# Gated linear recurrence with a squared-ReLU feed-forward: longer units, Q~ and K~ transposed on VectorE, static buffers and a planned order

## Chip, cores and metric

The kernel runs on one core of one Trainium2 chip. The metric is device time in microseconds (us) of that core, the median of several runs. A profile is one further execution of the same program, recorded by the hardware profiler.

## The reference, cut to what matters

```python
# q, k, v, a_re, a_im: (B=4, H=8, S=768, D=48), float32
mag   = np.sqrt(a_re * a_re + a_im * a_im)
scale = np.minimum(mag, 0.999) / (mag + 1e-06)
a_re_n, a_im_n = a_re * scale, a_im * scale
for t in range(S):                       # S_re, S_im: (B, H, D, D), start at 0
    ar, ai = a_re_n[:, :, t, :, None], a_im_n[:, :, t, :, None]
    new_re = ar * S_re - ai * S_im
    new_im = ar * S_im + ai * S_re
    S_re, S_im = new_re + einsum('bhd,bhe->bhde', k[:, :, t], v[:, :, t]), new_im
    y[:, :, t] = einsum('bhd,bhde->bhe', q[:, :, t], S_re)
x = y.transpose(0, 2, 1, 3).reshape(3072, 384)
h = x @ w_in                             # w_in: (384, 2048), float64
return (relu(h) ** 2 @ w_out)            # w_out: (2048, 384), float64
```

The decay of a step is a complex number for each batch, head and feature. With its running product P_t, the step-by-step sum becomes a masked product of matrices: y_t is the sum over s up to t of (q_t P_t) against (k_s / P_s), times v_s. The kernel calls the two scaled operands Q~ and K~; each has a real and an imaginary part, so 96 rows for a head.

## The kernel before

**Tiling.** A unit is half a batch: L = 384 steps of all 8 heads, `W` = 3 blocks of 128 steps. There are 8 units. A unit goes through three stages.

**Chain** (`chain_work`, mostly VectorE and ScalarE). Partition p holds the steps 3p, 3p+1, 3p+2. `load` brings a_re, a_im, q, k (L643) and v (L654), on SP's queue for the first two units and POOL's afterwards. `roots` and `normalise` scale the decays (L668 to L696), `inner` multiplies the three steps of a partition together (L706 to L711), `inverse` forms 1/P within a partition (L717 to L731), `totals` transposes the partition totals on TensorE (L770) so that `scan` can run over the 128 partitions, which then lie along the free dimension; it does so by 16 calls of `product`, each one complex product in 4 VectorE operations (L799 to L803). `back` transposes the result back (L835, copied by ScalarE at L836), and `apply` multiplies everything out: 10 operations for each half of the heads (L847 to L862), which leave Q~ and K~ in the tile QK with steps on partitions.

**Pairs** (`pair_work`), for each of 4 pairs of heads. `turn` transposes Q~ and K~ on TensorE (L890, 12 for a pair) and ScalarE copies them to SBUF (L891) as QKT, features on partitions. `score` multiplies K~ by Q~ (L900) and VectorE masks the result (L902). `keep` forms each block's contribution to the state, K~ by v (L917), and VectorE adds them up (L925, L927). For that product K~ must lie with consecutive steps on partitions; `apply` gets it there over DRAM (rows<-QK at L869, KC<-rows at L871, both on POOL's queue). `mix` (L936, L941) adds masked scores by v and Q~ by state in `ypair`, ScalarE copies that out (L944), and SP moves the rows into `xT` (L952), where features are on partitions and steps along the row.

**Dense.** `hidden` computes one tile of 128 hidden features for 384 steps in three passes (L971), ScalarE applies ReLU and squares (L976, L977). `project` accumulates 16 tiles for 128 steps (L985), ScalarE copies out (L989), SP stores (L991). The weights arrive as float64. `fetch` (L581) loads raw pieces, 16 for each matrix, `lower` (L589, ScalarE) and `convert` (L602 to L609, VectorE) turn them into float32. `inspect` reads the weights once more late in the kernel (L624 to L629) and looks for exponents out of range; `verdict` (L1013 to L1032) puts all guard values into one flag. If the flag is set, `general_path` computes everything again by another method.

**Order.** Buffers come from rotating pools, and a framework inserts the waits. The order within an engine is that in which the Python code emits the work. `merge` (L1035) interleaves lists in proportion to their lengths: after a start by hand (chain 0, pairs 0 with the w_in conversion, chain 1 followed by the hidden tiles of unit 0, pairs 1 with the w_out conversion, chain 2), turn n merges the dense work of unit n with the pairs of unit n+1 and the chain of unit n+2.

Of the kernel before, what the change touches and what calls it, by code (L numbers as in the profile page):

```python
# [9 lines left out]
F32 = mybir.dt.float32  # L10
# [469 lines left out]

@with_exitstack
def fast_path(ctx, tc, q, k, v, a_re, a_im, moe_w_in, moe_w_out, out, flag):

# [7 lines left out]
    W = 3  # L496
    L = W * C
    NHALF = S // L
# [5 lines left out]
    NF = FF // C  # L504
    SCALE = 2.0 ** 59
    HH = H // 2
    NU = B * NHALF

    dve, pool, act = nc.vector, nc.gpsimd, nc.scalar

    const = ctx.enter_context(tc.tile_pool(name="const", bufs=1))
    nat = ctx.enter_context(tc.tile_pool(name="nat", bufs=1))
    wk = ctx.enter_context(tc.tile_pool(name="wk", bufs=1))
    pr = ctx.enter_context(tc.tile_pool(name="pr", bufs=2))
    gp = ctx.enter_context(tc.tile_pool(name="gp", bufs=NF // 2))
    xp = ctx.enter_context(tc.tile_pool(name="xp", bufs=2))
    NRAW = 5
    wst = ctx.enter_context(tc.tile_pool(name="wst", bufs=NRAW))
    trp = ctx.enter_context(tc.tile_pool(name="trp", bufs=2, space=PSUM))
    scp = ctx.enter_context(tc.tile_pool(name="scp", bufs=2, space=PSUM))  # L520
    dram = ctx.enter_context(tc.tile_pool(name="dram", bufs=1, space=bass.MemoryType.DRAM))
    yp = ctx.enter_context(tc.tile_pool(name="yp", bufs=1, space=PSUM))
    dp = ctx.enter_context(tc.tile_pool(name="dp", bufs=3, space=PSUM))

    act.preload_act_table_set("natural_log_exp_and_others")

    def after(x, y):

        tc.add_manual_dep(x.ins, y.ins.name, NOSYNC, reason="order")


    ident = const.tile([C, C], F32, name="ident")
    make_identity(nc, ident)

    mask = const.tile([C, C], F32, name="mask")
    pool.memset(mask, 1.0)
    pool.affine_select(out=mask, in_=mask, pattern=[[1, C]], compare_op=ALU.is_ge,
                       fill=0.0, base=0, channel_multiplier=-1)
    mask3 = mask.unsqueeze(1).to_broadcast([C, NM, C])

    sums = const.tile([C, NU, 7], F32, name="sums")
    mark = {}
    grow = const.tile([C, NU, NM], F32, name="grow")
    total = const.tile([C, B, NM], F32, name="total")

    ypair = yp.tile([C, L], F32, name="ypair")
    dve.memset(ypair, 0.0)


    w1 = const.tile([C, NF, NM, C], F32, name="w1")
    w2 = const.tile([C, NF, DM], F32, name="w2")

    wide = moe_w_in.dtype != F32
    odd = const.tile([C, 2 * NF], F32, name="odd")

    def piece(i):
        words = 2 if wide else 1
        if i < NF:  # L560
            w_in = moe_w_in.bitcast(U32) if wide else moe_w_in
            return (w1[:, i].rearrange("p m f -> p (m f)"),
                    w_in[:, ts(i, words * C)].rearrange("(m p) f -> p m f", p=C))
        i -= NF
        w_out = moe_w_out.bitcast(U32) if wide else moe_w_out
        return w2[:, i], w_out[ts(i, C), :].unsqueeze(1)

    raws = {}
    AHEAD = 3

    def fetch(i):

        dst, src = piece(i)
        if not wide:
            nc.gpsimd.dma_start(
                out=dst.rearrange("p (m f) -> p m f", m=src.shape[1]), in_=src)
            return

        raw = raws[i] = (gp.tile([C, DM, 2], U32, name="raw", tag="g") if i < NF else
                         wst.tile([C, DM, 2], U32, name="raw", tag="raw"))  # L580
        get = (nc.sync if i >= NF + NRAW else nc.gpsimd).dma_start(  # L581
            out=raw.rearrange("p (m f) two -> p m (f two)", m=src.shape[1]), in_=src)
        after(get, mark["landed"])

    def lower(i):

        if wide:
            lo = raws[i][:, :, 0]
            op = act.activation(out=lo, in_=lo, func=AF.Copy, scale=2.0 ** -29)  # L589
            after(op, mark["last"])  # L590

    def convert(i):

        for j in range(i, i + AHEAD) if i % NF == 0 else [i + AHEAD - 1]:
            if j // NF == i // NF:
                lower(j)
        if wide:
            dst, _ = piece(i)
            more, hi = raws[i][:, :, 0], raws[i][:, :, 1]
            bits = dst.bitcast(U32)  # L600

            first = dve.tensor_scalar(out=bits, in0=hi, scalar1=0x07FFFFFF, scalar2=3,  # L602
                                      op0=ALU.bitwise_and, op1=ALU.logical_shift_left)

            after(first, mark["QK", int(i >= NF + NRAW)])
            dve.scalar_tensor_tensor(out=bits, in0=hi, scalar=0xC0000000, in1=bits,
                                     op0=ALU.bitwise_and, op1=ALU.bitwise_or)

            dve.tensor_tensor(out=bits, in0=bits, in1=more, op=ALU.add)  # L609
        n = i + (NF // 2 if i < NF else NRAW)  # L610
        if n < (NF if i < NF else 2 * NF):
            fetch(n)

    SPARE = ("fa0", "fa1", "fb0", "fb1")

    def inspect(i):


        if not wide:
            return  # L620
        _, src = piece(i)
        t = wk.tile([C, 2, HH, W, D], F32, name="look", tag=SPARE[i % 4])
        flat_t = t.rearrange("p r h c d -> p (r h c d)").bitcast(U32)[:, 0:2 * DM]
        nc.gpsimd.dma_start(  # L624
            out=flat_t.rearrange("p (m f) -> p m f", m=src.shape[1]), in_=src)
        hi = flat_t.rearrange("p (n two) -> p n two", two=2)[:, :, 1]
        dve.tensor_scalar(out=hi, in0=hi, scalar1=0x38000000, scalar2=0x78000000,
                          op0=ALU.bitwise_xor, op1=ALU.bitwise_and)
        dve.tensor_reduce(out=odd[:, i:i + 1], in_=hi, axis=AX, op=ALU.max)  # L629


    def load(u):
        def src(ap):
            return ap[u["b"], :, ts(u["half"], L), :]


        get = nc.sync if u["n"] < 2 else nc.gpsimd
        for name, pair in (("a", (a_re, a_im)), ("qk", (q, k))):
            for z in range(2):
                t = u[name, z] = nat.tile([C, 2, HH, W, D], F32, name=f"{name}{z}",  # L640
                                          tag=f"{name}{z}")
                for j, ap in enumerate(pair):
                    get.dma_start(  # L643
                        out=t[:, j].rearrange("p h c d -> p h (c d)"),
                        in_=src(ap)[ts(z, HH)].rearrange(LOADS, c=W))
        if u["n"] == 0:

            gate = const.tile([C, 2], F32, name="gate")
            pool.tensor_copy(out=gate[:, 0:1], in_=u["a", 0][:, 1, HH - 1, W - 1, D - 1:D])
            mark["landed"] = pool.tensor_copy(out=gate[:, 1:2],  # L650
                                              in_=u["a", 1][:, 1, HH - 1, W - 1, D - 1:D])
        u["v"] = pr.tile([C, NM, H, D], F32, name="v", tag="v")
        for j in range(W):
            get.dma_start(out=u["v"][:, j],  # L654
                          in_=src(v).rearrange("h (j s) d -> s j h d", s=C)[:, j])

    def flat(t):
        return t.rearrange("p h c d -> p (h c d)")

    def whole(t):  # L660
        return t.rearrange("p r h c d -> p (r h c d)")

    def roots(u, z):

        a, n = u["a", z], u["n"]
        fa = u["fa", z] = wk.tile([C, 2, HH, W, D], F32, name=f"fa{z}", tag=f"fa{z}")
        fb = u["fb", z] = wk.tile([C, 2, HH, W, D], F32, name=f"fb{z}", tag=f"fb{z}")
        square = act.activation(out=whole(fa), in_=whole(a), func=AF.Square,  # L668
                                accum_out=sums[:, n, z:z + 1])
        m2 = flat(fb[:, 0])  # L670
        dve.tensor_tensor(out=m2, in0=flat(fa[:, 0]), in1=flat(fa[:, 1]), op=ALU.add)
        f0, f1, t = flat(fa[:, 0]), flat(fa[:, 1]), flat(fb[:, 1])
        act.activation(out=f0, in_=m2, func=AF.Ln)
        act.activation(out=f1, in_=f0, func=AF.Exp, scale=-0.5)
        last = act.activation(out=t, in_=f1, func=AF.Square)
        dve.scalar_tensor_tensor(out=t, in0=m2, scalar=-0.5, in1=t,
                                 op0=ALU.mult, op1=ALU.mult)
        dve.scalar_tensor_tensor(out=t, in0=t, scalar=1.5, in1=f1,
                                 op0=ALU.add, op1=ALU.mult)
        if n == 0 and z == 0:  # L680
            mark["roots"] = last
        elif n == 0:
            after(square, mark["roots"])
# [438 lines left out]
```

## Time and profile before

| What | Value |
|---|---|
| Runs | 807.89, 809.83, 813.04 us; median 809.83 |
| Span of the profiled execution | 808.9 us |
| Instructions in it | 9895 |
| DMA traffic | 76.24 MB, of which HBM read 56.62 and written 14.16 |
| POOL's DMA queues | 55.85 MB, 21.3% of 16 engines' span |
| SP's DMA queues | 19.67 MB, 8.2% |
| Chain that ended last, shares | PE 38%, issue 20%, VectorE 11%, DMA 10%, ScalarE 8% |

The costliest groups of instructions follow, from the page's fifth part: line, engine, operation, result and operands, shape and count, then busy us, mean ns of one, and the engine's idle time just before them with what ended it. A matmul row has a duration of its own, but matmuls overlap one another in the array, so a row's mean is longer than the distance from one to the next.

```profile
L971 PE MATMUL h<-xT,w 128*128 128x384 f32 x768 | 271.7, 496 | 4.7 <-DMA xT<-yt 3.2
L985 PE MATMUL o<-w,g 128*128 128x384 f32 x768 | 265.2, 493 | 0.0
...
L891 ACT COPY QKT<-tq 96x512 f32<-96x512 f32 x96 | 79.3, 851 | 34.6 <-PE tq L890 34.6
...
L890 PE MATMUL tq<-ident,QK 128*96 128x128 f32 x384 | 59.8, 289 | 21.5 <-DVE QK L862 14.9
```

### The profile page before, as it was taken

The numbers are of one execution on the slowest core, as the hardware profiler recorded it, in microseconds if no ns is written. First come the engines' busy times: TensorE is split into PE (matmuls) and PEld (weight loads), VectorE is DVE, ScalarE is ACT, GpSimd is POOL, SyncE is SP. The second block draws the span as 40 slices with busy tenths as digits, with TensorE's granted clock in tenths as the row PEclk, the third lists the DMA queues.
The fourth block names the chain that finished last, engine by engine and source line by source line (L and its number), as shares of the span: only waits on it lengthen the run. The fifth ranks groups of instructions, "written<-read, shape, count | busy, mean of one in ns | idle before, by whom it ended". The sixth has DMA issues, their size and how long they took to land.

```text
span 808.9 us, 9895 instructions
## 1 busy us (share of the span) xinstructions
PE 708.7 (88%) x3474; PEld 461.0 (57%) x3474; DVE 519.0 (64%) x1332; ACT 398.4 (49%) x753; POOL 110.2 (14%) x162
## 2 busy tenths in 40 slices
PE   0138794689899999999999998999999999899997
PEld 0027452665466666666666665666566666566554
DVE  5898899966987994639582866469464866600000
ACT  5814594435568618931586138811893145212510
POOL 5003100401030013000500031002300044200000
PEclk9998997789999999999999999999999999999999
DMA  9429310642043026000800053002600188500000
GB/s 278 151 69 327 92 59 1 223 132 57 11 142 107 18 68 203 9 8 28 266 22 7 18 172 100 8 17 80 219 9 16 28 280 270 196 17 28 1 12 23
DMA packets 38747, 76.24 MB, mean 94 GB/s; under 512 B 10752, under 2 KB 25216, under 8 KB 38688
## 3 DMA queue, kind: packets, MB, share of 16 engines
q0 software_dynamic: 14608, 55.85, 21.3%
q1 hardware_dynamic: 24080, 19.67, 8.2%
q8 instruction: 29, 0.48, 0.2%
q14 instruction: 30, 0.25, 0.1%
HBM read 56.62 MB, written 14.16 MB: 88 GB/s over the span
## 4 chain that ended last, share of the span: by engine, by line
PE 38%; issue 20%; DVE 11%; DMA 10%; ACT 8%; POOL 1%; SPq 0%; POOLq 0%; ACTq 0%
PE o L985 18%; PE h L971 11%; DVE fa L799 3%; DMA a<-in_a_im_dram 2%; PE sa L900 2%; DMA look<-in_moe_w_out_dram 2%; DMA look<-in_moe_w_in_dram 2%; PE ypair L936 1%; ACT QKT L891 1%; PE ypair L941 1%; PE kv L917 1%; DMA rows<-QK 1%; DMA KC<-rows 1%; PE tq L890 1%; ACT g L976 1%
## 5 line engine op out<-in xcount | busy, mean ns | idle before, releaser
L971 PE MATMUL h<-xT,w 128*128 128x384 f32 x768 | 271.7, 496 | 4.7 <-DMA xT<-yt 3.2
L985 PE MATMUL o<-w,g 128*128 128x384 f32 x768 | 265.2, 493 | 0.0
L985 PEld LDWEIGHTS o<-w,g 128*128 128x128 f32 x768 | 141.1, 192 | 85.8 <-issue 4.7
L971 PEld LDWEIGHTS h<-xT,w 128*128 128x128 f32 x768 | 140.2, 193 | 84.9 <-issue 8.6
L891 ACT COPY QKT<-tq 96x512 f32<-96x512 f32 x96 | 79.3, 851 | 34.6 <-PE tq L890 34.6
L976 ACT ACTIVATE g<-h 128x384 f32<-128x384 f32 x128 | 61.6, 484 | 55.8 <-PE h L971 55.5
L890 PE MATMUL tq<-ident,QK 128*96 128x128 f32 x384 | 59.8, 289 | 21.5 <-DVE QK L862 14.9
L890 PEld LDWEIGHTS tq<-ident,QK 128*96 128x96 f32 x384 | 46.6, 134 | 43.9 <-issue 26.7
L902 DVE TENSOR_TENSOR A<-sa,mask 128x384 f32<-128x384 f32 x64 | 35.2, 552 | 52.1 <-PE sa L900 52.0
L977 ACT ACTIVATE g<-g 128x384 f32<-128x384 f32 x128 | 66.4, 522 | 2.1
L900 PEld LDWEIGHTS sa<-QKT 96*128 96x128 f32 x384 | 52.5, 199 | 15.6 <-ACT QKT L891 5.6
L900 PE MATMUL sa<-QKT 96*128 96x128 f32 x384 | 57.2, 288 | 3.0 <-ACT QKT L891 3.0
L944 ACT COPY yt<-ypair 112x384 f32<-112x384 f32 x32 | 15.2, 476 | 90.2 <-PE ypair L941 85.0
L869 POOL DMA_DIRECT2D rows<-QK x16 | 9.1, 566 | 338.0 <-DVE QK L862 338.0
L989 ACT COPY ot<-o 128x384 f32<-128x384 f32 x24 | 11.4, 476 | 84.0 <-PE o L985 84.0
L862 DVE TENSOR_TENSOR QK<-qk,a 128x576 f32<-128x576 f32 x64 | 44.3, 749 | 0.0
L936 PE MATMUL ypair<-A,v 128*48 128x128 f32 x384 | 38.7, 284 | 3.3 <-ACT yt L944 3.3
L770 PE MATMUL tot<-ident,last 128*128 128x128 f32 x72 | 14.3, 302 | 29.8 <-ACT last L730 25.7
L917 PEld LDWEIGHTS kv<-v,KC 128*96 128x96 f32 x320 | 32.5, 171 | 10.6 <-ACT QKT L891 3.6
L917 PE MATMUL kv<-v,KC 128*96 128x48 f32 x320 | 33.2, 252 | 3.8 <-DMA KC<-rows 3.2
L836 ACT COPY xn<-bk 128x384 f32<-128x384 f32 x24 | 11.1, 481 | 49.7 <-PE bk L835 49.7
L668 ACT ACTIVATE fa<-a 128x1152 f32<-128x1152 f32 x16 | 18.6, 1161 | 31.7 <-DMA a<-in_a_im_dram 31.7
(109 smaller groups left out, 887.7 us busy)
## 6 DMA issues: line engine op xcount, KB each, us to landing
rows<-QK POOLq DMA_DIRECT2D x16, 576.0 KB, 3.9
raw<-in_moe_w_in_dram POOLq DMA_DIRECT2D x16, 384.0 KB, 7.1
look<-in_moe_w_in_dram POOLq DMA_DIRECT2D x16, 384.0 KB, 4.9
look<-in_moe_w_out_dram POOLq DMA_DIRECT2D x16, 384.0 KB, 4.4
KC<-rows POOLq DMA_DIRECT2D x8, 576.0 KB, 5.5
out_dram<-ot SPq DMA_DIRECT2D x24, 192.0 KB, 1.9
raw<-in_moe_w_out_dram SPq DMA_DIRECT2D x11, 384.0 KB, 3.7
xT<-yt SPq DMA_DIRECT2D x48, 72.0 KB, 2.2
```

Source lines behind the costliest of these rows:

```text
L799: dve.tensor_tensor(out=t, in0=x, in1=y[:, j].unsqueeze(1).to_broadcast(shape), op=ALU.mult)
L862: done = dve.tensor_tensor(out=o[:, :, :, r * D:(r + 1) * D], in0=qk[:, j], in1=a[:, r], op=ALU.mult)
L890: nc.tensor.transpose(ps[:, 2 * j + h], src, ident)
L891: act.copy(out=u["T"][i].rearrange("r z (p c) -> r c z p", c=W)[:, c], in_=ps)
L900: nc.tensor.matmul(sa[:, j], lhsT=T[:, 2 + h, ts(j, C)], rhs=T[:, h, ts(j, C)], start=True, stop=True)
L902: dve.tensor_tensor(out=u["A"][i][:, h], in0=sa, in1=mask3, op=ALU.mult)
L917: nc.tensor.matmul(ps[:, j, h], lhsT=u["KC", hh // HH][:, j, hh % HH], rhs=u["v"][:, j, hh], start=True, stop=True)
L936: nc.tensor.matmul(ypair[64 * h:64 * h + D, ts(j, C)], lhsT=u["v"][:, j, 2 * i + h], rhs=A[:, h, j], start=True, stop=S_j is None)
L971: nc.tensor.matmul(ps, lhsT=w1[:, f, m], rhs=u["xT"][:, m], start=(m == 0), stop=(m == NM - 1))
L976: act.activation(out=t, in_=ps, func=AF.Relu)
L977: act.activation(out=t, in_=t, func=AF.Square)
L985: nc.tensor.matmul(u["o"], lhsT=u["g"][f][:, ts(c, C)], rhs=w2[:, f], start=(f == 0), stop=(f == NF - 1))
```

## The change

Nearly all of `fast_path` is written anew. What is computed, its types and the guards stay the same in kind.

- **Units of 512 steps.** `W` = 4, so partition p holds four consecutive steps and there are 6 units. They run across the ends of batches: `parts` splits the loads of a unit, `cross`, `fresh` and `ends` say where a batch ends inside or at the edge of a unit, and the scan starts anew there. `inner` has three steps where it had two. The partitions within a block of 128 steps are in an order of their own (step 4p+c of a block lies at row 32c+p of the operands), and the mask is built for that.
- **`product`** has 3 VectorE operations: a negated copy of the imaginary part is kept beside the real and imaginary ones, so that one operation adds both halves.
- **Transposes.** For units 0 and 1 (`EARLY` = 2) TensorE transposes as before (`turn_pe`, L1186, L1189). For units 2 to 5 `turn` makes two 32x32-block transposes on VectorE for each pair (L1163) and 12 moves within SBUF on SP's queue (L1167).
- **`gather`** (L1127) brings K~ to consecutive steps by 12 to 16 moves within SBUF for each half of the heads, in place of the two transfers over DRAM.
- **Loads.** a, q, k and v come on SP's queue in every unit. v comes in 16 pieces of 32 rows (L805) where it came in 3.
- **Dense.** Hidden tiles are for 256 steps: 1152 passes of 256 columns (L1296), two tiles side by side in one PSUM bank and one ReLU and square for both. An output block is stored in four transfers (L1323) where it was one, since its rows are in the order named above.
- **Weights.** Raw pieces are twice as large, 8 for each matrix, and land in places that are not yet in use: parts of `w2` and `g`, `vv[1]`, the QT buffers.
- **Static buffers.** Every SBUF and PSUM tile is allocated once, by name, and taken in turn by an index.
- **Order.** Each step is given to the class `Plan` with an assumed duration, what it reads and writes and a rank. `order` simulates all engines and queues with these durations; whenever an engine is free, the ready step of lowest rank goes next (pairs 1, chains 2, dense and conversion 3, inspection 5; unit number second). The steps are emitted in that order with the framework's own scheduling turned off.

The core of the diff:

```diff
+class Plan:
+    HOP = {"PE": 0.12, "DVE": 0.1, "ACT": 0.15, "POOL": 0.2, "SP": 0.05}
+    RATE = 280e3
...
+    def order(self):
...
+        for _ in steps:
+            best = None
+            for e in engines:
+                if not wait[e]:
+                    continue
+                t = max(free[e], min(at[n] for n in wait[e]))
+                if best is None or t < best[0]:
+                    best = (t, e)
+            t, e = best
+            n = min((n for n in wait[e] if at[n] <= t), key=lambda n: (steps[n][4], n))
...
+        return sorted(start, key=lambda n: (start[n], n))
+
+    def emit(self):
+        for n in self.order():
+            self.steps[n][3]()
...
-    W = 3
+    W = 4
     L = W * C
-    NHALF = S // L
+    NU = B * S // L
...
+    G = L // 2
+    EARLY = 2
...
+    NQT = 3
+    QT = [sb(f"QT{s}", 16 * C) for s in range(NQT)]
+    KC = [sb(f"KC{z}", W * HH * R) for z in range(2)]
+    vv = [sb(f"v{s}", W * H * D) for s in range(2)]
...
+    CHAIN, PAIR, DENSE, CONV, LATE = 2, 1, 3, 3, 5
...
+    raw1 = ([w2slot(s) for s in (3, 2, 1, 0)]
+            + [(gu[:, s * 2 * PW:(s + 1) * 2 * PW], ...) for s in range(3)]
+            + [(vv[1].bitcast(U32), [("v", 1)])])
+    raw2 = [w2slot(3), w2slot(2), w2slot(3), w2slot(2),
+            (QT[2].bitcast(U32)[:, 0:2 * PW], [("QT", 2)]),
+            (vv[1].bitcast(U32), [("v", 1)]),
...
-        for j in range(2):
-            t = whole(u["fa", j])[:, 0:n].rearrange(split, r=2, **sizes)
-            dve.tensor_tensor(out=t, in0=x, in1=y[:, j].unsqueeze(1).to_broadcast(shape),
-                              op=ALU.mult)
-            f.append(t)
-        dve.tensor_tensor(out=dst[:, 0], in0=f[0][:, 0], in1=f[1][:, 1], op=ALU.subtract)
-        dve.tensor_tensor(out=dst[:, 1], in0=f[0][:, 1], in1=f[1][:, 0], op=ALU.add)
+                dve.tensor_tensor(out=g1, in0=xx, in1=y(0, 1).to_broadcast(shape),
+                                  op=ALU.mult)
+                dve.tensor_tensor(out=g2, in0=xx[:, ::-1], in1=y(1, 3)[:, ::-1],
+                                  op=ALU.mult)
+                dve.tensor_tensor(out=dst, in0=g1, in1=g2, op=ALU.add)
...
-        nc.gpsimd.dma_start(out=rows.rearrange("(p c) e -> p (c e)", c=W),
-                            in_=out_k.rearrange("p c h e -> p (c h e)"))
-        nc.gpsimd.dma_start(out=kc[:, 0:n].rearrange("p j h e -> p j (h e)"),
-                            in_=rows.rearrange("(j p) e -> p j e", p=C)[:, 0:n])
+        queue = sp if n < EARLY else pool
+        for i in needs(n):
+            for c in range(W):
+                dma(queue, [("f", z, 2), ("f", z, 3)], [("KC", z)],
+                    lambda i=i, c=c: queue.dma_start(
+                        out=kc[32 * c:32 * c + 32, i], in_=nat[32 * i:32 * i + 32, c]), ...)
...
+        def turn(i):
+            T6 = aq[z].rearrange("p (y j x) -> p y j x", y=2, j=NJ)
+            for j in range(2):
+                step("DVE", tt(768), ..., lambda nat=nat, dst=dst, j=j:
+                     dve.transpose(out=dst[:, j], in_=nat), rank)
+            for b in range(W):
+                for j in range(NJ):
+                    dma(sp, ..., [("QT", s)], lambda b=b, j=j, z=z, t=t, T6=T6: sp.dma_start(
+                            out=t[32 * j:32 * j + 32, b],
+                            in_=T6[32 * b:32 * b + 32, i % 2, j]), rank, 65536, ...)
...
+        for i in range(NP):
+            (turn_pe if n < EARLY else turn)(i)
...
-        for m in range(NM):
-            nc.tensor.matmul(ps, lhsT=w1[:, f, m], rhs=u["xT"][:, m],
-                             start=(m == 0), stop=(m == NM - 1))
+                    for m in range(NM):
+                        pe.matmul(ps[:, j], lhsT=w1[:, f // FP, m, ts(f % FP, C)],
+                                  rhs=xT[:, m, base:base + G],
+                                  start=(m == 0), stop=(m == NM - 1))
...
-            nc.sync.dma_start(out=out[r:r + C, :], in_=t)
+            for c in range(W):
+                dma(sp, [("ot", o)], [], lambda c=c, o=o, dst=dst: sp.dma_start(
+                    out=dst[c], in_=ots[o][32 * c:32 * c + 32]), rank, 32 * DM * 4)
...
-        merge(*lists)
+    with tc.manual_schedule():
+        plan.emit()
+    verdict()
```

## The prediction

> **What bounds the kernel now.** I read the busy times, the 40 slices, then busy times by stretch, then single rows in order of time.
>
> ```profile
> PE 708.7 (88%) x3474; PEld 461.0 (57%) x3474; DVE 519.0 (64%) x1332; ACT 398.4 (49%) x753; POOL 110.2 (14%) x162
> ...
> PE   0138794689899999999999998999999999899997
> ...
> DVE  5898899966987994639582866469464866600000
> ```
>
> TensorE is nearly full from slice 8 on; before that VectorE is the full one. I cut the span where VectorE ends the second unit's chain (153.4 us), where the second unit's pairs end (181.2) and where the last dense part stands alone (740.8). Columns: stretch, length, then busy us (count) of PE, PEld, DVE, ACT, POOL, then clock, DMA share, GB/s.
>
> ```profile
> 0.00:153.40 153.40, 77.84 (x392) 52.82 (x392) 133.06 (x343) 85.45 (x160) 26.86 (x46) 0.91 0.46 142
> 153.40:181.20 27.80, 24.52 (x199) 18.89 (x199) 20.64 (x52) 10.79 (x19) 3.93 (x5) 0.88 0.58 184
> 181.20:740.80 559.60, 544.16 (x2693) 353.23 (x2692) 365.14 (x938) 284.02 (x539) 79.39 (x111) 0.99 0.27 86
> 740.80:803.10 62.30, 62.19 (x194) 36.10 (x192) 0.15 (x1) 17.69 (x36) 0.00 (x0) 1.00 0.03 11
> ```
>
> So there are two regimes: until 153.4 VectorE's serial chains set the pace and half of TensorE's time is lost; from then on TensorE's work does, with 19 us idle in 649.7. Prices come from rows in order of time (start, length, engine, line, ...):
>
> ```profile
> 771.86 31.12 PE L985 MATMUL o<-w,g 128*128 128x384 f32 x96
> ...
> 346.38 0.83 PE L900 MATMUL sa<-QKT 96*128 96x128 f32 x6
> 347.05 2.10 PE L971 MATMUL h<-xT,w 128*128 128x384 f32 x6
> 349.08 0.42 PE L936 MATMUL ypair<-A,v 128*48 128x128 f32 x4
> 349.34 0.39 PE L941 MATMUL ypair<-QKT,S 96*48 96x128 f32 x4
> 349.56 0.39 PE L936 MATMUL ypair<-A,v 128*48 128x128 f32 x4
> ...
> 143.89 2.75 DVE L862 TENSOR_TENSOR QK<-qk,a 128x576 f32<-128x576 f32 x4
> 146.56 1.42 DVE L850 TENSOR_TENSOR fa<-a,xn 128x576 f32<-128x576 f32 x2
> ...
> 2.40 0.51 SPq L643 DMA_DIRECT2D a<-in_a_im_dram  x1
> 2.95 0.51 SPq L643 DMA_DIRECT2D qk<-in_q_dram  x1
> ```
>
> What counts is the spacing of starts, not a row's length. A 384-column pass costs 31.12/96 = 0.324 us; six L900 passes take 0.67 until the next start, 0.112 each; four ypair passes 0.22, 0.055 each. Likewise read: L890 0.11, L917 0.10. Four 576-wide VectorE operations start 2.67 apart from the next: 0.67 each, which is 576/960 + 0.07. I price other widths n as n/960 + 0.07: 768 costs 0.87, 1536 costs 1.67, 512 costs 0.60. SP issues a transfer every 0.52-0.55.
>
> [...]
>
> **The change, part by part.**
>
> *TensorE work.* In back-to-back time the kernel before holds 1536 x 0.324 = 498 (dense), 384 x 0.112 = 43 (scores), 384 x 0.11 = 42 (Q~/K~ transposes), 320 x 0.10 = 32 (states), 704 x 0.055 = 39 (ypair), 144 x 0.112 = 16 (chain transposes): 670. The change turns 768 L971 passes of 384 columns into 1152 of 256: 0.324 x 256/384 = 0.216 each, again 249. Scores, states and ypair keep their counts (24 blocks of 128 either way). Transposes stay for units 0 and 1 only: 128 of 384, minus 28. Chain transposes go from 8 x 18 to 6 x 18, minus 4. New sum **638**, minus 32.
>
> *VectorE per unit.* Each half had 19 operations of 576, one of 1152 and two inner steps of 1.48: (12.7 + 1.27 + 2.96) x 2 = 33.9; now 19 of 768, one of 1536 and three inner steps: (16.5 + 1.67 + 4.44) x 2 = 45.3. The scan over products took 14.7 (from 120.57 to 137.5 without what lies between); 64 operations become about 33, and single ones widen to 768: I estimate 12.4. With the scan of x (1.5, now about 2.0) a chain costs 50.1 before and **59.7** after; eight cost 401, six 358.
>
> *The start.* In the built order VectorE must finish, before unit 1's chain is through: two chains 119.4, pairs of unit 0 (8 masks x 0.60 + 16 state sums x 0.18 = 7.8) and 5.6 of the 8 w_in pieces (2.2 each: 0.47 + 0.87 + 0.87), 12.3: together 139.5. Before it was 100.2 + 6.1 + 16 x 1.21 = 125.7, and took 153.4: 27.7 of gaps (loads, ScalarE's turns). With the same gaps the new end is 167; a walk op by op through the first 100 us, in which all eight w_in pieces have their own landing place and ScalarE doesn't stand behind a raw load as at 72-79 us, gives 154. I take **160**, bounds 152 and 170.
>
> *TensorE behind it.* By then it has done unit 0's attention (114/6 = 19, transposes 7), 4 of chain transposes, five hidden tiles (60 x 0.216 = 13) and 1 of unit 1's transposes: 44. Left: 594. In the kernel before 615 were left at 153.4 (1440 x 0.324 + 7/8 of 156 + 12) and took 649.7, so interleaving cost 34.5, or 4.9 for each of 7 units. Five units now: 24.5. Bounds 15 (less contention) and 42 (it goes with the work, not with the units, plus stalls).
>
> *The end.* The last output leaves in four transfers in place of one, three more issues, 1.6; 5.8 + 1.6 = 7.4.
>
> *Moved within SBUF.* Units 2 to 5: 32 VectorE transposes of 768, 0.87 each, 28 in all; [...]upper 3.5 (four times), never a gain. VectorE totals about 358 + 35 conversion + 47 pairs + 28 + 21 checks = 490, 110 at worst on top: beside 638 of TensorE, hidden. Each pair then needs 12 SP transfers: 12 x 0.52 + 2.2 (a 72 KB xT transfer lands in 2.2; bounds 1.9 and 5.5) = 8.4 us from transpose to scores. Per unit SP issues 48 of these, 10 xT, 8 to 16 loads, 16 v and 16 output transfers, about 100 x 0.52 = 52 us of some 110. The built order shows that each transfer also waits for the eighth before it; 8 x 0.52 is above 2.2, so that rarely binds. Queued behind a waiting transfer are others' QT and xT: unit 2's first QT stands behind outputs that need dense work of unit 0. TensorE has 18 us of hidden tiles between, against 2 + 8.4: covered. For a unit's third and fourth pair the cover is about 9 and 10 us against 8 to 10: a microsecond or two a unit, inside the 24.5. Loads of units 2 on leave POOL for SP; K's trip over DRAM (3.9 + 5.5 us) becomes 12 to 16 transfers (0.57 each, from the rows<-QK issues, then 2 to 5 landing), needed only after the scores. All at nothing; without cover they are the slow rival.
>
> *Static order and buffers* cost nothing where TensorE has dense work next in line: the built order ends with four groups, 165 us of pure dense work, so attention runs ahead.
>
> Sum: 160 + 594 + 24.5 + 7.4 = 786 of span, against 808.9. The median of the runs stands 0.9 above the span: **787**.
>
> **Rivals.**
> 1. *The start eats it*: VectorE ends at 170, v of unit 1 (its place is borrowed by a raw piece until then) comes late, interleaving 36: 170 + 594 + 36 + 7 = 807. For it: VectorE is full until 153 and does 14 us more; against: the gaps should shrink.
> 2. *Better than summed*: 152 + 594 + 15 + 7 = 768. For it: 165 us without interleaving at the end; against: the first pairs still alternate in short turns.
> 3. *Slower*: the QT transfers in SP's queue replace the transposes as a wait. If TensorE, which takes its instructions in order, stands half of the 8.4 us at each of 16 pairs, it is 787 + 67 = 854. It decides once SP's issue and landing for a pair exceed the 9 to 18 us of work placed between; half a doubling of the landing does it. Against: SP's rows are 0.34-0.67, landings 1.9-2.2.
> 4. *The change does not do what it says*: a guard value fails and the general path runs as well; over 1000. Guards are the same in kind.
>
> **How the numbers follow.** Main case 0.55 (775-798), rival 2 0.20, rival 1 0.15, rival 3 0.09, rival 4 0.01. One per cent, 8 us, is about what a measurement can tell from no change. Faster: main and rival 2, 0.75; same 0.15; slower 0.10. Range 763 to 815: it holds rivals 1 and 2 and leaves out 3 and 4.
>
> **What would show it.** TensorE busy falls to 660-680; 1152 hidden passes spaced 0.216; L1186 occurs 128 times; VectorE ends unit 1's products near 160, and TensorE has some 85-95 us idle before; afterwards under 30 idle, little of it on QT transfers; some 160 us of dense work alone at the end. I am wrong if VectorE's second chain ends past 175, if TensorE waits for QT or KC more than 40 us in sum, or if passes of 256 columns are spaced above 0.23.

## The result and the profile after

The changed kernel takes 851.58 us (median, 848.76 to 854.73) against 809.57 us before (807.89 to 813.04): ratio 1.0516, 95% interval 1.0474 to 1.0559. It is slower; the forecast was 787, range 763 to 815.

The page of the changed kernel: busy times, then the slices of TensorE, VectorE and TensorE's clock.

```profile
PE 680.8 (80%) x3566; PEld 517.5 (61%) x3566; DVE 516.5 (61%) x978; ACT 339.3 (40%) x577; POOL 78.2 (9%) x154
...
PE   0117743199988999979879898987899999999994
...
DVE  5998899955588977799259995779656100000000
...
PEclk9999977599999999989899999998899999999998
```

TensorE's busy time fell by 28 us to 680.8, just above the 660 to 680 that were forecast, yet there are gaps in its slices from 12 to 29, where the kernel before has one slice below 9. Both kernels over the same four stretches (length, then busy us and count of PE, PEld, DVE, ACT, POOL, clock, DMA share, GB/s), first the changed kernel, then the one before:

```profile
0.00:168.00 168.00, 57.59 (x408) 47.98 (x408) 147.81 (x289) 82.38 (x138) 12.51 (x31) 0.88 0.48 130
168.00:260.00 92.00, 87.49 (x506) 67.43 (x507) 59.58 (x95) 55.74 (x95) 2.17 (x3) 0.95 0.34 89
260.00:640.00 380.00, 338.89 (x1877) 259.50 (x1876) 293.34 (x573) 150.95 (x261) 58.70 (x114) 0.95 0.43 106
640.00:848.50 208.50, 196.81 (x778) 142.63 (x776) 15.74 (x25) 50.23 (x84) 4.86 (x6) 0.98 0.14 43
```

```profile
0.00:168.00 168.00, 90.47 (x524) 63.95 (x524) 144.49 (x371) 92.61 (x171) 30.79 (x51) 0.92 0.48 152
168.00:260.00 92.00, 87.05 (x394) 53.65 (x393) 73.93 (x181) 54.23 (x104) 11.24 (x15) 0.94 0.27 85
260.00:640.00 380.00, 371.51 (x1882) 243.92 (x1881) 252.43 (x677) 202.94 (x391) 44.75 (x60) 1.00 0.22 68
640.00:808.90 168.90, 159.68 (x680) 99.52 (x678) 48.14 (x106) 48.60 (x91) 23.40 (x36) 0.98 0.31 101
```

Busy time hides a part of the difference, because a row is longer than the spacing where runs of matmuls are short (in the kernel before, a row of six L900 passes at 346.38 us takes 0.83, and the next row starts 0.67 after it) or the clock is low (four passes of 384 columns at a clock of 0.57 take 2.57 us below, where four times 0.324 is 1.3). So I price the matmuls that start in each stretch at the prediction's spacings ("work"); the rest of the stretch is "loss":

| us | work, whole span | loss 0-168 | 168-260 | 260-640 | 640-end | span |
|---|---|---|---|---|---|---|
| before | 670.6 | 97.9 | 14.3 | 14.3 | 11.8 | 808.9 |
| after | 638.2 | 123.4 | 10.0 | 65.6 | 11.3 | 848.5 |

The work fell by 32.4, as the prediction summed. The loss rose by 72: 25 at the start and 51 in the middle. What TensorE waits for in the middle (engine, line, what ended the wait; us in total, times, longest):

```profile
PE tr L922 <- DVE e L993: 15.8, 4, 4.4
PE sc L1203 <- DMA QT<-aq: 14.7, 12, 3.5
PE d L1296 <- ACT g L1303: 5.2, 3, 3.1
PE tr L922 <- DVE x L963: 1.9, 3, 1.5
```

L922 are the transposes within a unit's chain, waiting for VectorE's products; the second line is scores waiting for the moved Q~ and K~. All waits of this view sum to 41 us. A part of the rest shows in the clock that TensorE was granted. One wait for L993, and the windows around it:

```profile
480.14 1.49 PE L922 MATMUL tr<-ident,e 128*128 128x128 f32 x6 [3.88 <-DVE e L993]
481.42 2.57 PE L1314 MATMUL d<-w,g 128*128 128x384 f32 x4
```

```profile
476.00:480.00 4.00, 0.26 (x1) 0.00 (x0) 3.86 (x9) 0.00 (x0) 0.00 (x0) 1.00 0.09 22
480.00:484.00 4.00, 3.86 (x11) 2.80 (x12) 3.93 (x9) 0.96 (x2) 0.00 (x0) 0.57 0.00 0
484.00:488.00 4.00, 4.00 (x20) 3.51 (x20) 3.93 (x6) 1.80 (x4) 0.00 (x0) 1.00 0.20 49
```

In the first window TensorE is nearly idle. After the stall of 3.9 us the clock of the next 4 us is 0.57, and four passes of 384 columns take 2.4 us until the next row, where 4 x 0.324 = 1.3 was to be expected. These four stood behind L922 in the order and did not run during the stall, though their operands were there: ScalarE had last written g at 461.98, and the passes up to the stall add to the same output block. Summed over windows of 4 us from 168 to 640, TensorE is idle 45.6 us, and busy time times the missing clock gives 20.2; in the kernel before (153.4 to 740) the two are 18.7 and 8.0.

### The profile page after: what moved, and what is told of

Same layout as the page of the kernel before. It is cut to its first block, busy times and chain, and to the rows that moved or that the text cites. A ratio compares the mean times of both kernels' runs of the same rounds, so it can differ in the third digit from the quotient of the medians.

```text
span 848.5 us, 10163 instructions
## 1 busy us (share of the span) xinstructions
PE 680.8 (80%) x3566; PEld 517.5 (61%) x3566; DVE 516.5 (61%) x978; ACT 339.3 (40%) x577; POOL 78.2 (9%) x154
## 4 chain that ended last, share of the span: by engine, by line
PE 42%; DVE 27%; SPq 8%; DMA 8%; ACT 6%; issue 4%; DVEq 0%; ACTq 0%; POOLq 0%
PE d L1314 18%; PE d L1296 17%; SPq L1167 5%; PE sc L1203 3%; DVE f L989 3%; DVE f L991 2%; DVE f L863 2%; DVE e L993 2%; DMA aq<-in_a_im_dram 2%; DMA QT<-aq 2%; DVE f L1091 2%; DVE f L1102 2%; DMA xT<-yt 1%; PE tr L1219 1%; DVE w L747 1%
## 5 line engine op out<-in xcount | busy, mean ns | idle before, releaser
L1296 PE MATMUL d<-xT,w 128*128 128x256 f32 x1152 | 268.6, 391 | 26.0 <-ACT g L1303 8.0
L1296 PEld LDWEIGHTS d<-xT,w 128*128 128x128 f32 x1152 | 222.7, 196 | 64.5 <-ACT g L1303 10.0
L1314 PE MATMUL d<-w,g 128*128 128x384 f32 x768 | 260.0, 494 | 1.5 <-DVE w L747 1.5
L1314 PEld LDWEIGHTS d<-w,g 128*128 128x128 f32 x768 | 146.0, 193 | 97.4 <-issue 4.5
L1303 ACT ACTIVATE g<-d 128x512 f32<-128x512 f32 x96 | 57.1, 595 | 138.0 <-PE d L1296 115.9
L1127 POOL DMA_DIRECT2D KC<-f x104 | 50.9, 498 | 375.8 <-DVE f L1102 188.1
L1203 PE MATMUL sc<-QT 96*128 96x128 f32 x384 | 52.2, 285 | 15.5 <-DMA QT<-aq 14.7
L1304 ACT ACTIVATE g<-g 128x512 f32<-128x512 f32 x96 | 60.6, 631 | 3.1
L1203 PEld LDWEIGHTS sc<-QT 96*128 96x128 f32 x384 | 48.6, 196 | 20.5 <-issue 15.4
L1318 ACT COPY ot<-d 128x384 f32<-128x384 f32 x24 | 11.5, 477 | 123.4 <-PE d L1314 120.2
L1206 DVE TENSOR_TENSOR A<-sc,mask 128x512 f32<-128x512 f32 x48 | 32.4, 686 | 39.8 <-PE sc L1203 39.8
L922 PE MATMUL tr<-ident,xn 128*128 128x128 f32 x54 | 10.3, 306 | 43.0 <-ACT xn L894 39.7
L1102 DVE TENSOR_TENSOR f<-aq 128x768 f32<-128x768 f32 x48 | 42.9, 954 | 0.4
L922 PE MATMUL tr<-ident,e 128*128 128x128 f32 x36 | 9.2, 427 | 42.1 <-DVE e L993 42.1
L863 DVE TENSOR_TENSOR f<-aq 128x384 f32<-128x384 f32 x72 | 37.0, 555 | 1.0
L922 PEld LDWEIGHTS tr<-ident,xn 128*128 128x128 f32 x54 | 6.8, 152 | 46.7 <-issue 29.1
L922 PEld LDWEIGHTS tr<-ident,e 128*128 128x128 f32 x36 | 6.8, 218 | 44.6 <-DVE e L993 44.6
```

The lines of the kernel that those rows point to most:

```text
L863: dve.tensor_tensor(out=f, in0=a[:, :, :, c - 1], in1=a[:, j, :, c].unsqueeze(1).to_broadcast([C, 2, HH, D]), op=ALU.mult)
L1102: lambda j=j, r=r, o=o: dve.tensor_tensor(out=o[:, :, :, r * D:(r + 1) * D], in0=qk[:, j], in1=a[:, r], op=ALU.mult), rank)
L1127: lambda i=i, c=c: queue.dma_start(out=kc[32 * c:32 * c + 32, i], in_=nat[32 * i:32 * i + 32, c]),
L1203: pe.matmul(sa[:, j], lhsT=T[:, j, 1, h], rhs=T[:, j, 0, h], start=True, stop=True)
L1296: pe.matmul(ps[:, j], lhsT=w1[:, f // FP, m, ts(f % FP, C)], rhs=xT[:, m, base:base + G], start=(m == 0), stop=(m == NM - 1))
L1303: act.activation(out=o, in_=ps, func=AF.Relu)
```

## Experiments

All edits are made on the changed kernel unless a base is named. The table gives each median, its ratio to the kernel before on the same chip, the loss per stretch as above, and the waits between 260 and 640 us of the chain's transposes (L922) and of scores for moved tiles (QT). Losses and waits are those of the one profiled execution; that of e11 took 809.54 us, 5 above its median. The work is 638 in each, 666 where all transposes are on TensorE (e2, e7, e10).

| Run | median | ratio [95%] | 0-168 | 168-260 | 260-640 | 640-end | L922 | QT |
|---|---|---|---|---|---|---|---|---|
| changed kernel | 851.58 | 1.052 [1.047, 1.056] | 123 | 10 | 66 | 11 | 19.7 | 14.7 |
| e1 dense 0.65 | 878.84 | 1.086 [1.080, 1.093] | 123 | 9 | 56 | 52 | 1.7 | 11.3 |
| e2 all on PE | 850.54 | 1.051 [1.045, 1.058] | 123 | 14 | 37 | 10 | 18.9 | - |
| e3 w_in first | 844.79 | 1.044 [1.036, 1.052] | 106 | 21 | 68 | 9 | 19.3 | 14.0 |
| e4 e3 + e1 | 873.78 | 1.084 [1.076, 1.092] | 107 | 22 | 59 | 45 | 3.4 | 11.5 |
| e5 loads on POOL | 838.04 | 1.035 [1.030, 1.040] | 123 | 8 | 56 | 10 | 20.4 | 9.3 |
| e6 e5 + e1 | 865.51 | 1.067 [1.063, 1.072] | 123 | 7 | 49 | 50 | 10.1 | 0.8 |
| e7 e2 + e1 | 840.42 | 1.037 [1.032, 1.041] | 123 | 7 | 20 | 22 | 5.6 | - |
| e8 e5 + durations | 806.47 | 0.998 [0.996, 1.001] | 106 | 14 | 37 | 10 | 5.6 | 7.3 |
| e9 e8 + all conv. first | 778.88 | 0.965 [0.958, 0.972] | 95 | 4 | 30 | 10 | 1.8 | 11.1 |
| e10 as e9, all on PE, loads on SP | 792.81 | 0.981 [0.974, 0.988] | 94 | 3 | 19 | 9 | 2.8 | - |
| e11 durations alone | 804.79 | 0.994 [0.992, 0.997] | 106 | 14 | 34 | 15 | 0.2 | 3.7 |
| e12 all conv. first alone | 835.02 | 1.032 [1.026, 1.039] | 96 | 9 | 77 | 11 | 18.4 | 13.2 |
| e13 VectorE durations | 838.44 | 1.036 [1.029, 1.042] | 123 | 13 | 50 | 12 | 3.4 | 18.1 |
| e14 ScalarE durations | 840.46 | 1.038 [1.031, 1.044] | 118 | 9 | 63 | 10 | 17.9 | 14.7 |
| e15 SP duration | 825.92 | 1.021 [1.014, 1.028] | 106 | 18 | 50 | 12 | 18.8 | 0.5 |
| e16 e11 + all conv. first | 781.17 | 0.964 [0.958, 0.971] | 96 | 3 | 31 | 10 | 4.2 | 4.6 |

### First theories: the order's dense steps, the moves, the start

e1, both dense steps:

```diff
-                step("PE", 1.3, ...
+                step("PE", 0.65, ...
```

> Only the duration that the plan assumes for one dense step is changed, from 1.3 to the 0.65 us that three passes of 256 or two of 384 columns take in the trace (3 x 0.216, 2 x 0.324). Theory A, the plan puts too little dense work between the steps of the chains and TensorE arrives early: between unit 1's pairs and the last dense part TensorE loses 66 us now; that falls to 25-35 and the median to 805-820 us. Theory B, the transposed tiles moved by SP's queue are late whatever the order: the loss stays above 50 and the median above 838. Theory C, only the start costs: 846-856.

It took 878.84, worse by 27. The premise was wrong: the trace has two rows for each float32 matmul (1152 rows of L1296 for 12 groups x 16 tiles x 3 matmuls), so a dense step is six passes of 256 columns, 1.30 us, and the plan had it right. Believing dense work to be twice as fast, the order put more of it ahead of a chain's transposes and scores: the waits for L922 all but went (19.7 to 1.7), the loss in the middle fell by 9 only. Slices of TensorE and VectorE in e1, and rows of TensorE before one set of scores:

```profile
PE   0107754299999999969999869998789998569995
...
DVE  5998878963373881676664266784663684560000
...
453.06 19.51 PE L1314 MATMUL d<-w,g 128*128 128x384 f32 x60
472.41 1.95 PE L1203 MATMUL sc<-QT 96*128 96x128 f32 x16
```

VectorE works until slice 36, with holes: up to 18.8 us at a time it waits for scores (L1206 behind L1203) that stand behind dense work. The chain of the last unit ends at 732.5 (603.2 in the changed kernel), its attention comes when the dense work of the other units is used up (83 us, its own, follow it), and the loss moves to the end (52).

e2 (all units by `turn_pe`):

```diff
-            (turn_pe if n < EARLY else turn)(i)
+            turn_pe(i)
```

> All units are transposed on TensorE and copied by ScalarE, as units 0 and 1 are; no 32x32 transposes on VectorE, no moves within SBUF by SP. TensorE gets 256 transposes, 28 us, more. Theory A: the 15 us of waits for QT go, the waits for the chain (E L993, xn) stay, the new work partly fills idle time: 845-870. Theory B (QT in SP's queue is the cause of the 66 us): the loss in the middle halves and the median is 825-842 in spite of the added 28.

850.54: the loss in the middle falls by 29, and TensorE's work rises by 28. Both ways of transposing cost the same here. The waits for L922 are hardly touched (18.9), so the moves are at most one of two causes.

e3 and e4 (conversions of w_in ranked ahead of unit 1's chain; e4 with e1's edit too):

```diff
-        rank = (CONV, i)
+        rank = (CHAIN, 0.5) if i < NPIECE else (CONV, i)
```

> The conversions of w_in get a rank ahead of unit 1's chain, so that the 16 hidden tiles of the first group can run while VectorE is in that chain. TensorE did 60 passes of hidden tiles by the end of that chain, and could do 96 to 192. VectorE ends the chain 6-7 us later. Theory A and C: 8 to 25 us of dense work moves into idle time of the start, the median falls to 828-845. If the start were free (what is gained is given back in the middle): 848-856.

> Both: dense step 0.65 us in the plan, and conversions of w_in ahead of unit 1's chain. Theory A: the gains add, 780-802 us, below the kernel before. Theory B: above 825.

e3: 844.79, just inside the gain that was expected. The loss up to 168 falls by 17; the next stretch gives 11 back: unit 1's chain now ends at 181.0 in place of 167.2 and its transposes wait 9.7 us for it, and projections wait 7.8 us for w_out, still converted after the chain. e4: 873.78, a miss like e1 and from the same wrong premise.

### The queue of the loads

In the middle, SP's queue in order of time (start, time until the last issue, line, count):

```profile
385.26 15.38 SPq L1167 DMA_DIRECT2D QT<-aq  x24
400.69 2.58 SPq L792 DMA_DIRECT2D aq<-in_a_re_dram  x2
403.37 6.27 SPq L1167 DMA_DIRECT2D QT<-aq  x10
409.74 1.17 SPq L1267 DMA_DIRECT2D xT<-yt  x2
```

24 moves take 15.4 us, 0.64 each, and the next unit's a_im follows only after 48 moves (it is issued at 422). e5 moves the loads of a, q, k:

```diff
-        queue = sp
+        queue = sp if n < EARLY else pool
```

> a, q, k of units 2 to 5 are issued on POOL's queue, as in the kernel before, not on SP's behind the moves of Q~ and K~. Theory D (a unit's chain ends, its 48 moves take SP some 35 us, and the next unit's a stands behind them in the queue): VectorE starts the next chain 10-20 us earlier, the distance between the ends of two chains falls from 97-108 us to 85-95. TensorE's stalls in the middle stay (its order is still made with 1.3 us a dense step), so the median falls little: 838-852. Theory D2 (the wait is for the buffer aq, which the moves read, not for the queue): the distance stays above 97 and the median at 848-856.

> As e5_loads_pool, and 0.65 us for a dense step in the plan. In e1_durations the distance between chains grew to 124-146 us, above the 106 us of work that a unit is for TensorE, and dense work ran out before the last unit's attention came. Theory D: the distance falls by 10-20 to 105-125, and the median from 879 to 825-855. Theory D2: 865-880.

> As e2_all_on_pe (all transposes on TensorE, so neither moves on SP nor aq held by them), with 0.65 us for a dense step in the plan. In e2 the distance between chains was 93 us in the middle, below TensorE's 111 us for a unit. If the loop over moves and loads (theory D or D2) is what made e1 slow, TensorE is now nearly always full after 168 us: 168 + 621 of work + 20-35 + 12 = 820-836. If a right duration for dense work hurts for another reason, it is slower than e2 here too: 860-885.

e5: 838.04, at the edge of what was expected, and the ends of later chains (rows of L1102) lie 91, 104 and 91 us apart in place of 97, 108 and 100: less than the 10 to 20 us that were expected. The queue is not all: on POOL the loads still wait for the moves out of `aq`, 41 us in ten waits between 260 and 640, which is the wait of theory D2. L922 stays at 20. So queue and buffer held VectorE up, but that is not what makes the chain's transposes wait. e6 (865.51) lies in the range of D2, not of D, and e7 (840.42) in neither of its ranges; both halve a duration that was right. With more dense work between, the order with moved tiles loses 50 at the end, the one without 22.

### The plan's durations

VectorE in order of time in the changed kernel: an inner step (L863 to L869) and products of 192 columns (L989, L991, L993):

```profile
445.50 1.02 DVE L863 TENSOR_TENSOR f<-aq 128x384 f32<-128x384 f32 x2
446.56 0.36 DVE L867 TENSOR_TENSOR aq<-f 128x192 f32<-128x192 f32 x1
446.84 0.35 DVE L869 TENSOR_TENSOR aq<-f 128x192 f32<-128x192 f32 x1
447.22 1.03 DVE L863 TENSOR_TENSOR f<-aq 128x384 f32<-128x384 f32 x2
...
467.03 0.50 DVE L989 TENSOR_TENSOR f<-e 128x192 f32<-128x192 f32 x1
467.45 0.50 DVE L991 TENSOR_TENSOR f<-e 128x192 f32<-128x192 f32 x1
467.98 0.50 DVE L993 TENSOR_TENSOR e<-f 128x192 f32<-128x192 f32 x1
468.52 0.50 DVE L989 TENSOR_TENSOR f<-e 128x192 f32<-128x192 f32 x1
```

An inner step takes 447.22 - 445.50 = 1.72 us, the plan has 1.48; a product takes 468.52 - 467.03 = 1.49, the plan has 3 x (192/960 + 0.07) = 0.81. The plan gives each operation its width over 960 and 0.07 us, 0.27 at 192 columns. L869, which does not need L867's result, starts 0.28 after it; the next L863, which needs L869's, starts 0.38 after that. In a product L991 needs nothing of L989 and still starts 0.42 later, and each dependent step takes 0.53 or 0.54. So an operation that needs the one before it starts some 0.11 later, and those of this product are slower by some 0.15 each at the same width, for a reason that no run here shows. ScalarE's rows of 512 columns (L1303, L1304) have means of 0.595 and 0.631, the plan has 0.55. SP's issue is 0.64 against 0.52. So VectorE and SP are later on the chip than in the plan, and TensorE, whose order is fixed, comes to L922 and L1203 too early. e8 lengthens these on e5, with one figure for all products and one for all ScalarE operations; e9 and e10 add early conversion of all weights:

```diff
-        return n / 1200.0 + 0.12
+        return n / 1200.0 + 0.19
...
-        step("SP" if q is sp else "POOL", 0.52 if q is sp else 0.8,
+        step("SP" if q is sp else "POOL", 0.63 if q is sp else 0.8,
...
-                step("DVE", 2 * tt(m) + 2 * tt(m // 2), ...
+                step("DVE", 2 * tt(m) + 2 * tt(m // 2) + 0.27, ...
...
-            step("DVE", 3 * tt(cnt), reads, ...
+            step("DVE", 3 * tt(cnt) + 0.4, reads, ...
```

```diff
-        rank = (CONV, i)
+        rank = (CHAIN, 0.5)
```

> Correction to what stands with e1_durations: a dense step issues six passes of 256 or four of 384 columns, 6 x 0.216 = 4 x 0.324 = 1.30 us, so the plan's 1.3 was right and e1, e4, e6, e7 halved a right duration. Here, on e5_loads_pool, the durations that the trace shows to be too short are lengthened: a product by 0.4 us (1.48 against 0.81 at 192 columns), an inner step by 0.27 (1.72 against 1.48), each ScalarE step by 0.07, SP's issue from 0.52 to 0.63. Theory F (TensorE meets the chain's transposes too early because the chain is slower than planned): waits of transposes L922 after 260 us fall from about 20 us to under 8, the median from 838 to 822-832. If F is wrong: 834-842.

> e8_measured_dur and all conversions, w_in and w_out, ranked ahead of unit 1's chain. Theory S (the start costs 29 us more than before because dense work of unit 0 can't run while VectorE is in the second chain: hidden tiles lack w_in, projections lack w_out, and the buffers g fill): VectorE ends the chain near 190, but TensorE is busy from about 115 on; loss before the end of that chain falls from 123 to 80-90 in spite of the longer chain; median 790-815. Against S, the gain is given back because all later chains come 20 us later and the last unit's attention ends later, or pieces of w_out land too late: 825-840.

> e2_all_on_pe with the lengthened durations of e8 and all conversions ahead of unit 1's chain: no 32x32 transposes. Theory S and F: 666 of TensorE work, 80-90 of loss in the start, 30 in the middle, 12 at the end: 795-820. The difference to e9 is what the transposes on VectorE are worth once the start is out of the way: 28 us less work against their waits, so e10 minus e9 is 0 to 15 us.

e8 came out at 806.47, below its 822 to 832: the durations also moved conversions into the start (loss 106). e9, 778.88, and e10, 792.81, are below their ranges too (790 to 815, 795 to 820). Without 32x32 transposes TensorE has 28 us more work and loses 12 less, and the medians differ by 14, inside the 0 to 15 expected. The loads differ as well, on POOL in e9 and on SP in e10; e16 below has them on SP.

e11 and e12 make the two edits alone, on the changed kernel as it is.

> The changed kernel with the lengthened durations of e8 alone; a, q, k still on SP's queue. In e8 they took 32 us off e5. Theory F, the durations act by themselves: 815-825. If they help only where the loads are out of SP's queue: 838-850.

> The changed kernel with all conversions ahead of unit 1's chain and nothing else. In e9 this took 28 us off e8; w_in alone (e3) took 7 off the changed kernel. Theory S, the start's loss is a matter of its own: 820-830. If a better start is given back where TensorE meets the chains too early: 840-850.

e11: 804.79, 47 us off by numbers in the plan and nothing else, more than the expected 815 to 825 allowed; no operation of an engine is added or removed, only the order differs. TensorE's waits from 260 to 640 in e11:

```profile
PE d L1296 <- ACT g L1303: 8.8, 4, 3.1
PE d L1296 <- ACT ot L1318: 7.8, 2, 4.9
PE sc L1203 <- DMA QT<-aq: 3.7, 5, 1.0
PE sc L1203 <- issue: 0.6, 1, 0.6
PE tr L922 <- DVE e L993: 0.2, 1, 0.2
```

L922 went from 19.7 to 0.2, QT from 14.7 to 3.7. With e8 at 806.47, moving the loads adds nothing once the durations are right. e12: 835.02, a little above the expected 820 to 830. The start gains 27, the middle gives 12 back.

e13 to e15 split e11's edit: VectorE, ScalarE, SP.

> On the changed kernel, only product + 0.4 us and inner step + 0.27 us in the plan. If these carry the middle: waits of L922 after 260 us fall from 20 to under 5, loss between 260 and 640 us from 66 to 35-48, the start stays, 822-835. If not: 846-855.

> On the changed kernel, only ScalarE's steps + 0.07 us in the plan. Some 20 such steps stand in one chain, a little over 1 us a unit: 844-853. If ScalarE's part of the chain is what the plan had wrong: 825-838.

> On the changed kernel, only SP's issue 0.63 in place of 0.52 us in the plan. Unit 1's loads then come later in the plan and the conversions of w_in slip ahead of its chain, as in e3: the start's loss falls by some 12-17 us, and in the middle TensorE meets the tiles QT later, waits for them fall from 15 to under 8: 825-838. If it does the start alone: 838-846.

> e11_dur_alone and all conversions ahead of unit 1's chain; loads still on SP. If right durations and early conversions add and the loads' queue doesn't matter, as e8 against e11 says: 775-785, as e9. If the loads matter here: 790-805.

TensorE's waits from 260 to 640, first e13, then e15:

```profile
PE sc L1203 <- DMA QT<-aq: 18.1, 13, 3.4
...
PE tr L922 <- ACT xn L894: 2.0, 2, 1.7
PE tr L922 <- DVE e L993: 1.4, 2, 1.1
```

```profile
PE tr L922 <- DVE e L993: 15.4, 4, 4.2
...
PE sc L1203 <- DMA QT<-aq: 0.5, 1, 0.5
```

Each edit removes the wait that it describes and leaves the other: VectorE's durations take L922 from 19.7 to 3.4 while QT stays (18.1); SP's take QT from 14.7 to 0.5 while L922 stays (18.8). Their gains in the middle, 15 and 16, make up the 31 of e11. e13 missed its ranges by little (838.44 against 822 to 835, a loss of 50 against 35 to 48). e15's 826 (expected 825 to 838) has the start in it too: later loads in the plan leave VectorE a place for w_in ahead of the chain (106 against 123), of which the next stretch returns 8. e14 came out between its two ranges (840.46; 844 to 853 and 825 to 838); 5 of its 11 us lie in the start. The three gains, 13 + 11 + 26, add to about e11's 47.

e16: 781.17 (expected 775 to 785), ratio 0.964 [0.958, 0.971]. With e9 it beats both kernels. Against e10, whose loads are on SP too, it takes 12 us less: that is what the 32x32 transposes are worth in this order. Its slices:

```profile
PE 665.4 (85%) x3566; PEld 509.3 (65%) x3566; DVE 516.1 (66%) x978; ACT 339.6 (44%) x577; POOL 77.9 (10%) x154
...
PE   0115836999999999998999998999799899999994
...
DVE  4999988979488994298981499951889856400000
```

From slice 8 on TensorE has only small holes, and the loss at the start (96) is that of the kernel before (98).

## Why the prediction was wrong

**The step that failed** is the sentence that static order and buffers "cost nothing where TensorE has dense work next in line", and with it the 24.5 us for interleaving (bounds 15 to 42). It measured 75.6 (10.0 + 65.6): 51 of the 62.5 us by which the span of 848.5 exceeds the 786 of the sum; the start has 7 and the end 4. Dense work existed, but not next in line: the built order keeps it for the end, where 176 us of it stand alone (660.7 to 836.6). I read the 165 us of pure dense work that I saw there as a cover. They show that attention runs ahead and say nothing of the middle: e10 keeps 180 us for the end and loses 19 between 260 and 640, where the changed kernel loses 66. The 4.9 us per unit came from a kernel whose lists are merged a whole unit apart, and does not carry over to an order that places each step at the moment at which its plan believes the input to be ready. e13 and e15 show which beliefs were wrong; with them mended 48 us remain after the start (14 + 34, e11), so that 27 of the 51 are gone, and with early conversion too 34 (3 + 31, e16), the first just above the bounds and the second inside them. That e16's 781 lies near the forecast of 787 is in part chance: its start loses 96 where the sum has 116 (160 less 44), the rest loses 44 where the sum has 32.

**Start.** VectorE ended unit 1's chain at 167.2, forecast 160 (152 to 170). The gaps were right: it was idle for 20.2 us up to then, and the sum has 20.5. It was busy for 147.0 in place of 139.5. The scan was estimated at 12.4 and takes 13.4 (467.0 to 480.5 in a later unit), an inner step takes 1.72 where 1.48 was used; two scans and twelve inner steps make 5 of these 7.5 us. The work of TensorE done by then, 44 us, was right. What I had wrong in this part is its weight: I took the work that TensorE has done by then as given, where the order decides it. e12 and e16 show 27 us to be had.

**End.** The end is 11.3 against 7.4.

**Right:** the work (638.2 against 638); passes of 256 columns at 0.216 (96 from 671.08 to 691.80); L1186 128 times; a 32x32 transpose of 768 at 0.87 (four from 383.39 to 386.87), the value taken from n/960 + 0.07. That formula was my estimate from the 0.67 of L862 at 576 columns; it gives 0.27 at 192 and 1.67 at 1536, and the changed kernel has 0.28 (L867 at 446.56) and 1.67 (L848 at 443.83).

**Rival 3** gave 854, but its mechanism carries only a part of it: waits for QT are 14.7 us, some 16 of loss with what follows them, where it had 67. The 12 x 0.52 in its price was 12 x 0.64. That its time met the result is a coincidence. None of my three signs of being wrong occurred (chain past 175, over 40 us of waits for QT or KC, passes above 0.23): they covered the parts that I had priced and not the order. Of what was to show that I was right, TensorE's idle time failed: 110 us before the end of unit 1's chain (85 to 95 forecast) and 58 after it (under 30).

**Open:** units of 512 and static buffers were not tried by themselves. The 34 us that e11 still loses between 260 and 640 were not split further; of its 21 us of waits there, 16.6 are hidden passes behind ScalarE (L1303, L1318; 6.7 in the changed kernel). And no run lengthened a duration beyond what was measured. The figures used are rough, 0.4 us for every product where the trace is above the plan by 0.68 at 192 columns, 0.35 at 48 and 0.24 at 768, so these runs do not tell whether the plan must be right or only not too short.

## What to carry to other kernels

TensorE kept to the planned order even while the next step was not ready and a later one was (3.9 us before L922 at 480.14), so a planned order's wrong durations can turn into stalls: mending them took 47 us off (e11). So compare the plan's assumed durations with the trace's distances between starts, dependent small operations and DMA issues first, before anything else is judged. A long stretch of pure work at the end of an order is no cover for stalls earlier in it: here 176 us of it stood behind 65.6 us of loss between 260 and 640. A cost of interleaving measured under one ordering scheme is no price for another: 24.5 us were priced and 75.6 measured.

## What was not expected of the hardware

In the changed kernel a lowered clock of TensorE did not follow long stalls alone. It followed a wait of 1.4 us among short matmuls (scores for moved tiles, ending at 413.7):

```profile
411.00:414.00 3.00, 1.57 (x12) 1.35 (x11) 0.00 (x0) 0.00 (x0) 0.00 (x0) 1.00 0.50 125
414.00:418.00 4.00, 4.00 (x33) 4.00 (x32) 2.14 (x5) 0.00 (x0) 0.00 (x0) 0.67 0.38 88
418.00:422.00 4.00, 4.00 (x35) 3.88 (x36) 1.26 (x5) 0.00 (x0) 0.00 (x0) 0.50 0.46 110
...
437.00:441.00 4.00, 0.94 (x5) 0.58 (x4) 2.66 (x3) 3.94 (x8) 0.00 (x0) 1.00 0.89 143
441.00:445.00 4.00, 3.42 (x17) 2.68 (x16) 3.93 (x4) 3.97 (x7) 0.00 (x0) 1.00 0.58 95
```

With TensorE busy 1.57 of 3 us, the next windows have clocks of 0.67 and 0.50 although TensorE is busy all the time. Yet after a wait of 3.1 us that ended at 440.4, with 0.94 of 4 us busy, the clock stayed at 1.00. So the length of one wait does not settle it, and what does stays open. In sums over windows the lost clock is a third to nearly half of the idle time in this kernel: 20.2 us with 45.6 idle, in e11 10.7 with 32.4.
